# Gated Fourier and feed-forward mix: where the feed-forward share waits for the Fourier share, and when the first down step is loaded

## The chip, the cores and the metric

The kernel runs on one NeuronCore of one Trainium2 chip. The metric is the device time of one execution in microseconds (us), the median of several runs on the same chip. TensorE does the matrix products (PE in the profile; its weight loads are PEld), VectorE (DVE) and ScalarE (ACT) work on tiles in the on-chip memories, GpSimd (POOL) and SyncE (SP) here mostly issue transfers (DMAs) between these memories and the chip's main memory.

## The reference, cut to what matters

```python
def reference(A_x, A_dft_seq_re, A_dft_seq_im, A_dft_hid_re, A_dft_hid_im, B_x, B_w_gate, B_w_up, B_w_down, gate_w):
    def _A_ref(x, dft_seq_re, dft_seq_im, dft_hid_re, dft_hid_im):
        a = jnp.einsum("bsd,ed->bse", x, dft_hid_re)
        b = jnp.einsum("bsd,ed->bse", x, dft_hid_im)
        return jnp.einsum("ts,bse->bte", dft_seq_re, a) - jnp.einsum("ts,bse->bte", dft_seq_im, b)
    def _B_ref(x, w_gate, w_up, w_down):
        return (_gelu(x @ w_gate) * (x @ w_up)) @ w_down
    x = A_x
    g = _sigmoid((x * gate_w).sum(-1, keepdims=True))
    a = _A_ref(x, dft_seq_re, dft_seq_im, dft_hid_re, dft_hid_im)
    b = _B_ref(x, w_gate, w_up, w_down)
    return g * a + (1 - g) * b
```

x has 2048 tokens of 640 numbers, and the feed-forward part is 1728 wide. All is in 32-bit floats. The output is thus the sum of two shares: the Fourier share times g and the feed-forward share times 1 - g, with one g per token.

## The kernel before

**Tiles.** The 2048 tokens stand in four tiles of 512 (NT), worked in two pairs (tp = 0 and 1, t = 0 and 1 within a pair). The 640 columns are five blocks of 128 (the index e or d; ND = 5). The feed-forward width is 13 blocks of 128 and a rest of 64. A matrix product in 32-bit precision is done in three passes (`mm3`, L82): each operand is split into a high part, copied by ScalarE (`high`, L72), and a low part, which VectorE subtracts (`low`, L75); then TensorE does high by high (L84), high by low (L85) and low by high (L86). Many products are grouped into two-by-two schemes that save a product for some additions; their banks are called X, Z, V, L and Q, R, Y. TensorE's results land in eight banks of 128 x 512 in its accumulator memory (`bank`, L69). Operands take slots of 4 KB a partition out of 48 (`slot`, L63), small ones a tile out of 12 (`mtile`, L66).

**Stages.** First come the feed-forward blocks: a plain one and blocks f = 1 to 12, each for both pairs in seven steps (`gate_up`, L273). A step ends where the generator yields; in its steps VectorE adds or multiplies banks into the tiles s1, s2 and s5 (L298 after the third product bank V, L302 for X, L306 to L322 for the end), ScalarE applies the activation, and `keep` (L245) stores the hidden blocks and some differences of them to main memory, in hA and hT, from GpSimd's queue. At the end of block 11 the gates are worked out (`gate_rows`, L364), and the two tiles gm with 1 - g are loaded.

Then comes the down projection: 26 steps (`kseq`), for each pair seven with the products X, Z, V, L and seven with X, Q, R, Y; one in each second seven has nothing of its own to load. A step's weights (kw) and its two hidden halves (kr, 512 KB each, in two names that end in 0 and 1) are loaded by `load_k` (L450) from SyncE's queue; `split_k` (L478) makes their high parts kh and kb..h on ScalarE and their low parts kl and kb..l on VectorE; `step_k` (L535) does the products. Name 000 in kw000 or kb0000 is pair 0, first seven, step 0. When a bank set is complete, `put` (L541) multiplies a result by 1 - g and GpSimd stores it to accd, a scratch array in main memory for the feed-forward share.

Then follow the Fourier transform along the tokens (`cseq`; x parts xn loaded by `load_xn`, transform matrices by `load_c`, results u stored to uA and uT), and the one along the columns, with the output: 20 steps `useq`, five for each of pair 0 first half, pair 0 second half, pair 1 second half and, last, pair 1 first half. `fetch_mix` (L884) loads the tile gw with g and the pair's feed-forward share from accd into the tiles av; `mix` (L899) multiplies a result by g and adds it into av; `give` (L904) stores av to the output from GpSimd's queue. The last five steps are the part behind L987: `tail` (L991) runs the products of one bank over all five steps, so that the banks X, Z, V, L are ready one after the other, and each is multiplied, added into av and stored while the next one is worked out. The last bank is done in two halves, `yLast` being the second.

**What sets the order.** Each engine works through its instructions in program order. From `split_k(1)` on (L710), ScalarE and VectorE keep the order in which the code is written (`in_order`, L91). Ahead of it a scheduler orders each engine's instructions by what they wait for and by how early they are written. Work that is not urgent is put in a list `after` and written out at the next `late()`. SyncE's and GpSimd's transfers go out in their queues' order; a load into a slot waits until the slot's last reader is done.

**Where the first down step stands.** In block 12, `load_k(0)` to `load_k(2)` are written after steps 4 to 6 of the seven, `split_k(0)` after step 6; `split_k(1)` and `load_k(3)` follow when the block is written.

## Time and profile before

| | |
|---|---|
| runs | 1042.45, 1039.55, 1042.14 us; median 1042.14 us |
| profiled execution, first to last instruction | 1041.0 us |
| bytes read from and written to main memory | 173.93 MB, 63.98 MB |
| transfers of the hardware queue (issued by SyncE) | 174.22 MB |
| transfers of the software queue (issued by GpSimd) | 63.73 MB |

The profile is of one further execution. Its rows give, for a group of instructions of one line, engine and form, the busy time and mean duration; a row of a single instruction begins with its start in us from the span's start, then its duration, engine, line, operation and tiles (result <- operands). In brackets stands how long the engine stood idle just before it, and what it waited for. For a transfer there are three times in ns, for its issue, and then how long after issue it landed. "Granted clock" is the share of TensorE's full clock that it was given in the stretch.

### The profile page before, as it was taken

The page shows a single profiled execution, that of the slowest core. Times are in us where ns is not written, and L with a number is a line of the kernel's source. Part 1 is how long each engine was busy: PE and PEld are TensorE (multiplying, and loading weights), DVE is VectorE, ACT ScalarE, POOL GpSimd, SP SyncE. Part 2 cuts the span into 40 slices and gives each one's busy share as a digit, 9 for nine tenths or more (in the row PEclk, how much of TensorE's full clock was granted, in tenths as well). Part 3 has the DMA queues.
Part 4 walks back from the last instruction along what each step waited for, and adds up shares of the span by engine and source line. Part 5 has one row for each costly group of instructions (what it writes and reads, how often), then busy time and mean ns, then how long its engine had stood idle before and what let it go on. Part 6 is the DMA issues. An engine that isn't in the chain of part 4 may idle for free.

```text
span 1041.0 us, 12806 instructions
## 1 busy us (share of the span) xinstructions
PE 1026.8 (99%) x4523; PEld 848.6 (82%) x4523; DVE 785.4 (75%) x1051; ACT 448.8 (43%) x568; POOL 125.7 (12%) x237
## 2 busy tenths in 40 slices
PE   7999999999999899999999999999999999999997
PEld 5888888888888788888888888888888888888886
DVE  4898775767653966996798976696578769697888
ACT  5453333333532645655445443433344344354430
POOL 0012121212121200010010011001100200020011
PEclk9999999999999899999999999999999999999999
DMA  7146655647445977877866668467756777897762
GB/s 285 59 141 206 212 184 193 210 168 252 153 147 206 385 270 252 299 253 248 307 234 202 218 202 308 160 207 233 257 179 220 276 270 276 310 358 234 253 236 112
DMA packets 78753, 238.77 MB, mean 229 GB/s; under 512 B 10240, under 2 KB 18080, under 8 KB 78688
## 3 DMA queue, kind: packets, MB, share of 16 engines
q1 hardware_dynamic: 59408, 174.22, 49.4%
q0 software_dynamic: 19280, 63.73, 16.3%
q8 instruction: 35, 0.57, 0.2%
q14 instruction: 30, 0.25, 0.1%
HBM read 173.93 MB, written 63.98 MB: 229 GB/s over the span
## 4 chain that ended last, share of the span: by engine, by line
PE 65%; issue 21%; POOL 5%; DVE 5%; DMA 2%; ACT 1%; SPq 0%; POOLq 0%; ACTq 0%
PE pL L86 3%; PE pX L86 3%; PE pX L85 3%; PE pL L85 3%; PE pX L84 3%; PE pL L84 3%; POOL hA L246 2%; POOL hT L246 2%; PE pZ L86 1%; PE pV L86 1%; PE pY L86 1%; PE pY L85 1%; PE pR L86 1%; PE pR L85 1%; PE pQ L86 1%
## 5 line engine op out<-in xcount | busy, mean ns | idle before, releaser
L73 ACT ACTIVATE ch<-csa 128x1024 fp32r<-128x1024 f32 x32 | 34.0, 1062 | 88.8 <-DVE csa L431 53.7
L131 ACT ACTIVATE s<-pX 128x512 f32<-128x512 f32 x64 | 37.8, 596 | 73.2 <-PE pX L86 71.2
L73 ACT ACTIVATE ch<-cra 128x1024 fp32r<-128x1024 f32 x32 | 33.9, 1058 | 47.9 <-DVE cl L76 17.3
L76 DVE TENSOR_TENSOR cl<-cra,ch 128x1024 fp32r<-128x1024 f32 x32 | 39.1, 1222 | 17.6 <-ACT ch L73 16.8
L76 DVE TENSOR_TENSOR cl<-crb,ch 128x1024 fp32r<-128x1024 f32 x32 | 39.1, 1221 | 16.2 <-ACT ch L73 11.4
L85 PE MATMUL pL<-cl,xah 128*128 128x512 f32 x128 | 49.8, 389 | 0.0
L86 PE MATMUL pL<-ch,xal 128*128 128x512 f32 x128 | 49.8, 389 | 0.0
L298 DVE TENSOR_TENSOR s<-s,pV 128x512 f32<-128x512 f32 x24 | 16.3, 684 | 44.0 <-issue 24.4
L84 PE MATMUL pL<-ch,xah 128*128 128x512 f32 x128 | 49.3, 389 | 0.0
L246 POOL DMA_DIRECT2D hA<-s x48 | 26.0, 542 | 177.8 <-DVE s L308 171.4
L76 DVE TENSOR_TENSOR cl<-csb,ch 128x1024 fp32r<-128x1024 f32 x32 | 39.1, 1223 | 6.3 <-ACT ch L73 4.7
L73 ACT ACTIVATE ch<-crb 128x1024 fp32r<-128x1024 f32 x32 | 33.8, 1056 | 22.2 <-DVE cl L76 9.0
L76 DVE TENSOR_TENSOR cl<-csa,ch 128x1024 fp32r<-128x1024 f32 x32 | 39.1, 1222 | 4.0 <-ACT ch L73 3.3
L73 ACT ACTIVATE ch<-csb 128x1024 fp32r<-128x1024 f32 x32 | 33.9, 1059 | 11.9 <-PE pL L85 6.9
L76 DVE TENSOR_TENSOR kl<-kw,kh 128x1024 fp32r<-128x1024 f32 (+1 forms) x26 | 31.4, 1208 | 8.5 <-ACT kh L73 8.5
L307 ACT ACTIVATE s<-s 128x512 f32<-128x512 f32 x24 | 15.2, 634 | 39.1 <-DVE s L306 39.1
L73 ACT ACTIVATE kh<-kw 128x1024 fp32r<-128x1024 f32 (+1 forms) x26 | 27.3, 1048 | 7.8 <-DMA kw<-wsd 3.5
L299 ACT ACTIVATE s<-s 128x512 f32<-128x512 f32 x24 | 15.1, 630 | 31.7 <-DVE s L298 31.7
L85 PEld LDWEIGHTS pL<-cl,xah 128*128 128x128 f32 x128 | 24.0, 188 | 5.0
L84 PEld LDWEIGHTS pL<-ch,xah 128*128 128x128 f32 x128 | 24.0, 188 | 5.0
L86 PEld LDWEIGHTS pL<-ch,xal 128*128 128x128 f32 x128 | 24.0, 188 | 4.9
L771 POOL DMA_DIRECT2D uA<-s x16 | 8.6, 540 | 160.1 <-DVE s L817 153.3
(3564 smaller groups left out, 3356.8 us busy)
## 6 DMA issues: line engine op xcount, KB each, us to landing
cra<-in_ct SPq DMA_DIRECT2D x64, 512.0 KB, 4.1
crb<-in_ct SPq DMA_DIRECT2D x64, 512.0 KB, 4.7
hA<-s POOLq DMA_DIRECT2D x48, 256.0 KB, 4.4
hT<-s POOLq DMA_DIRECT2D x48, 256.0 KB, 5.4
kr<-hA SPq DMA_DIRECT2D x24, 512.0 KB, 7.8
kr<-hT SPq DMA_DIRECT2D x24, 512.0 KB, 6.5
ux<-uA SPq DMA_DIRECT2D x24, 512.0 KB, 5.2
ux<-uT SPq DMA_DIRECT2D x16, 512.0 KB, 5.6
```

What stands on the lines that cost most here:

```text
L73: nc.scalar.activation(hi, raw, AF.Copy)
L76: nc.vector.tensor_tensor(lo, raw, hi.bitcast(F32), op=ALU.subtract)
L84: nc.tensor.matmul(ps, lh, rh, start=first, stop=False, skip_group_check=True)
L85: nc.tensor.matmul(ps, lh, rl, start=False, stop=False, skip_group_check=True)
L86: nc.tensor.matmul(ps, ll, rh, start=False, stop=last, skip_group_check=True)
L131: nc.scalar.activation(m, src, AF.Copy)
L246: nc.gpsimd.dma_start(to[:, i], src)
L298: tt(s1, s1, V, op=ALU.add)
L299: nc.scalar.activation(s1, s1, AF.Gelu_apprx_tanh)
L307: nc.scalar.activation(s2, s2, AF.Gelu_apprx_tanh)
L771: nc.gpsimd.dma_start(to[:, i], src)
```

## The change

It does three things.

First, the feed-forward share is not kept in accd. `put` stores it directly into the output array, and accd goes.

Second, the Fourier share is put on by adding stores. `give` now multiplies a result by g, and GpSimd issues a store with `accum_op=ALU.add`, which adds the tile to what stands in the output. So the loads of av from accd and VectorE's additions into av go. Both tiles gw are loaded ahead of the output stage. In the last stage the results of bank X are added to the partial sums of pair 1 (ya, yc, ys), bank X itself is kept by a ScalarE copy (yx), Z and V are added to these, and each sum is multiplied by g and given by an adding store. Only the last column block (e = 4) of pair 1 is handled as before: its two tiles of feed-forward share are read back from the output into av (256 KB each), added on VectorE and stored plainly.

Third, `load_k(0)` is written at the end of block 11, right behind the loads of gm, `split_k(0)` after step 1 of block 12, and `load_k(1)` to `load_k(3)` after its steps 4 to 6.

```diff
--- before.py
+++ after.py
@@ -114,7 +114,6 @@
     uA, uT = ([[dram.tile([P, 4, T], F32, tag=f"u{n}{j}{p}", name=f"u{n}{j}{p}") for p in range(ND)] for j in range(2)] for n in "AT")
     grd, gmd = (dram.tile([1, S], F32, tag=n, name=n) for n in ("grd", "gmd"))
     wsd = [dram.tile([P, 8, P], F32, tag=f"wsd{k}", name=f"wsd{k}") for k in range(NK)]
-    accd = [dram.tile([P, ND, T], F32, tag=f"accd{t}", name=f"accd{t}") for t in range(NT)]
 
     def pair(dt, name):
         return slot(dt, [P, 2, T], name)
@@ -541,7 +540,7 @@
         def put(e, t, src):
             def do():
                 tt(src, src, gm[tp][:, t], op=ALU.mult)
-                nc.gpsimd.dma_start(accd[2 * tp + t][:, e], src)
+                nc.gpsimd.dma_start(out[2 * tp + t, e], src)
 
             after.append(do)
 
@@ -690,10 +689,11 @@
         for step in range(7):
             for w in work:
                 next(w)
-            if f == NF - 1 and step >= 4:
-                load_k(step - 4)
-                if step == 6:
+            if f == NF - 1:
+                if step == 1:
                     split_k(0)
+                if step >= 4:
+                    load_k(step - 3)
         if f % 2:
             sum_wd(f // 2)
         elif f <= 2 * ND:
@@ -701,6 +701,7 @@
         if f == NF - 2:
             gate_rows()
             gm = [gate_tile(gmd, tp, f"gm{tp}") for tp in range(2)]
+            load_k(0)
         for _ in range(2):
             if f > 1 and zq:
                 load_z(zq.pop(0))
@@ -709,7 +710,7 @@
     order.enter_context(in_order(ACT, DVE))
     split_k(1)
     for i in range(len(kseq)):
-        if i + 3 < len(kseq):
+        if 3 < i + 3 < len(kseq):
             load_k(i + 3)
         if i + 2 < len(kseq):
             split_k(i + 2)
@@ -881,34 +882,15 @@
 
     bk = {}
 
-    def fetch_mix(tp):
-
-        g = gate_tile(grd, tp, f"gw{tp}")
-        av = {}
-        for t in range(2):
-            for k in range(2):
-                a = pair(F32, f"av{tp}{t}{k}")
-                nc.sync.dma_start(a, accd[2 * tp + t][:, 2 * k : 2 * k + 2])
-                av[2 * k, t], av[2 * k + 1, t] = a[:, 0], a[:, 1]
-        a = pair(F32, f"av{tp}4")
-        for t in range(2):
-            nc.sync.dma_start(a[:, t], accd[2 * tp + t][:, 4])
-            av[4, t] = a[:, t]
-        return g, av
-
-    def mix(tp, e, t, v):
-        g, av = gav[tp]
-        tt(v, v, g[:, t], op=ALU.mult)
-        tt(av[e, t], av[e, t], v, op=ALU.add)
-
-    def give(tp, e, t):
-        nc.gpsimd.dma_start(out[2 * tp + t, e], gav[tp][1][e, t])
+    def give(tp, e, t, v):
+        tt(v, v, gw[tp][:, t], op=ALU.mult)
+        nc.gpsimd.dma_start(out[2 * tp + t, e], v, accum_op=ALU.add)
 
     def banks(names, n):
         for name in names:
             bk[name] = [bank(f"y{name}{n}{q}") for q in range(2)]
 
-    gav = {0: fetch_mix(0)}
+    gw = [gate_tile(grd, tp, f"gw{tp}") for tp in range(2)]
     for i, (tp, b, p) in enumerate(useq[: 3 * ND]):
         n = f"{tp}{b}"
         m = i - 2 * ND
@@ -944,11 +926,9 @@
 
             def mixed_y(tp=tp, cs=[sv["c11", q] for q in range(2)], ls=ls):
                 for q in range(2):
-                    mix(tp, 2 * q, 0, cs[q])
-                    give(tp, 2 * q, 0)
+                    give(tp, 2 * q, 0, cs[q])
                 for t in range(2):
-                    mix(tp, 4, t, ls[t])
-                    give(tp, 4, t)
+                    give(tp, 4, t, ls[t])
 
             after.append(mixed_y)
             continue
@@ -975,16 +955,15 @@
             for q in range(2):
                 s2, c21, c22 = es[q]
                 for e, t, v in ((2 * q, 1, s2), (2 * q + 1, 0, c21), (2 * q + 1, 1, c22)):
-                    mix(tp, e, t, v)
-                    if tp == 0:
-                        give(tp, e, t)
-
-        after.append(mixed_y)
-    last_mix = after.pop()
+                    give(tp, e, t, v)
+
+        if tp == 0:
+            after.append(mixed_y)
+    g = gw[1]
+    av = pair(F32, "av")
+    for t in range(2):
+        nc.sync.dma_start(av[:, t], out[2 + t, 4])
     late()
-    gav[1] = g, av = fetch_mix(1)
-    last_mix()
-    last = useq[3 * ND :]
     banks("XZVL", "last")
     Bs = [uks[3 * ND + p] for p in range(ND)]
 
@@ -996,19 +975,18 @@
     X, Z, V, L = (bk[name] for name in "XZVL")
     for q in range(2):
         tail(X[q], ("A11", q, True), 0)
-        x1, x2 = mtile(F32, f"yx1{q}"), mtile(F32, f"yx2{q}")
-        for t, v in ((0, x1), (1, x2)):
-            tt(v, X[q], g[:, t], op=ALU.mult)
-            tt(av[2 * q + 1, t], av[2 * q + 1, t], v, op=ALU.add)
-            give(1, 2 * q + 1, t)
-            tt(av[2 * q, t], av[2 * q, t], v, op=ALU.add)
+        s2, c21, c22 = es[q]
+        es[q] = copy(X[q], f"yx{q}"), s2
+        for t, v in enumerate((c21, c22)):
+            tt(v, v, X[q], op=ALU.add)
+            give(1, 2 * q + 1, t, v)
+        tt(s2, s2, X[q], op=ALU.add)
     for ps, w, b, t in ((Z, "S4", 3, 1), (V, "A12", 2, 0)):
         for q in range(2):
             tail(ps[q], (w, q, True), b)
-            v = mtile(F32, f"y{w}{q}")
-            tt(v, ps[q], g[:, t], op=ALU.mult)
-            tt(av[2 * q, t], av[2 * q, t], v, op=ALU.add)
-            give(1, 2 * q, t)
+            v = es[q][t]
+            tt(v, v, ps[q], op=ALU.add)
+            give(1, 2 * q, t, v)
     for t in range(2):
         parts = 2 if t else 1
         for c in range(parts):
@@ -1018,7 +996,7 @@
             tail(ps, ("e5", 1, False), 2 + t, cols)
             v = mtile(F32, f"yl{t}{c}")[:, : T // parts]
             tt(v, ps, g[:, t, cols], op=ALU.mult)
-            tt(v, v, av[4, t][:, cols], op=ALU.add)
+            tt(v, v, av[:, t, cols], op=ALU.add)
             (nc.sync if t else nc.gpsimd).dma_start(out[2 + t, 4, :, cols], v)
     order.close()
```

Behind line 117 the line numbers of the changed kernel are one lower, further back by 2 to 22.

VectorE at the end of block 12, before: s1, s2 and s5 are the block's tiles (the digits 12_0 and 12_1 are block and pair), pV, pX and pZ its banks, kl000 the low part of the first down step's weights and kb0000l that of its first hidden half.

```order
L298 TENSOR_TENSOR s112_0_2639<-s112_0_2639,pV12_0_2632 128x512
L298 TENSOR_TENSOR s112_1_2650<-s112_1_2650,pV12_1_2643 128x512
L302 TENSOR_TENSOR s512_2629<-s512_2629,pX12_0_2630 128x512
L302 TENSOR_TENSOR s512_2629<-s512_2629,pX12_1_2641 128x512
L306 TENSOR_TENSOR s212_0_2678<-s212_0_2678,pZ12_0_2631 128x512
L308 TENSOR_TENSOR s212_0_2678<-s212_0_2678,s512_2629 128x512
L306 TENSOR_TENSOR s212_1_2686<-s212_1_2686,pZ12_1_2642 128x512
L312 TENSOR_TENSOR s211_0_2509<-s212_0_2678,s211_0_2509 128x512
L314 TENSOR_TENSOR s511_2460<-s212_0_2678,s511_2460 128x512
L76 TENSOR_TENSOR kl000_2806<-kw000_2724,kh000_2805 128x1024
L308 TENSOR_TENSOR s212_1_2686<-s212_1_2686,s512_2629 128x512
L319 TENSOR_TENSOR s112_0_2639<-s112_0_2639,pX12_0_2630 128x512
```

The same place of the changed kernel:

```order
L297 TENSOR_TENSOR s112_0_2642<-s112_0_2642,pV12_0_2635 128x512
L76 TENSOR_TENSOR kl000_2676<-kw000_2625,kh000_2675 128x1024
L297 TENSOR_TENSOR s112_1_2653<-s112_1_2653,pV12_1_2646 128x512
L76 TENSOR_TENSOR kb0000l_2680<-kr0000_2628,kb0000h_2679 128x1024
L76 TENSOR_TENSOR kb0001l_2684<-kr0001_2630,kb0001h_2683 128x1024
L301 TENSOR_TENSOR s512_2632<-s512_2632,pX12_0_2633 128x512
L301 TENSOR_TENSOR s512_2632<-s512_2632,pX12_1_2644 128x512
L305 TENSOR_TENSOR s212_0_2693<-s212_0_2693,pZ12_0_2634 128x512
```

The low parts kl000, kb0000l and kb0001l stood behind the L308 and L322 operations of the block's end (kb0001l behind the rows shown); now all three stand ahead of the two additions of pX (L301).

ScalarE at the same place, before: copies of banks (L131, L291), the activations (L299, L307) and high parts (L73).

```order
L131 ACTIVATE s212_0_2678<-pX12_0_2630 128x512
L131 ACTIVATE s212_1_2686<-pX12_1_2641 128x512
L299 ACTIVATE s112_0_2639<-s112_0_2639 128x512
L299 ACTIVATE s112_1_2650<-s112_1_2650 128x512
L307 ACTIVATE s212_0_2678<-s212_0_2678 128x512
L73 ACTIVATE kh000_2805<-kw000_2724 128x1024
L307 ACTIVATE s212_1_2686<-s212_1_2686 128x512
L73 ACTIVATE kb0000h_2809<-kr0000_2727 128x1024
L73 ACTIVATE kb0001h_2813<-kr0001_2729 128x1024
```

ScalarE at that place now:

```order
L130 ACTIVATE s212_0_2693<-pX12_0_2633 128x512
L130 ACTIVATE s212_1_2701<-pX12_1_2644 128x512
L290 ACTIVATE s512_2632<-pZ12_0_2634 128x512
L290 ACTIVATE s512_2632<-pZ12_1_2645 128x512
L73 ACTIVATE kh000_2675<-kw000_2625 128x1024
L298 ACTIVATE s112_0_2642<-s112_0_2642 128x512
L73 ACTIVATE kb0000h_2679<-kr0000_2628 128x1024
L73 ACTIVATE kb0001h_2683<-kr0001_2630 128x1024
L298 ACTIVATE s112_1_2653<-s112_1_2653 128x512
```

The three high parts of the first down step, of which kh000 stood among the last activations and the others behind them, now stand around the activation of s1 (L298), ahead of both of s2 (L306).

VectorE in the last stage, at the first results of bank X, before: yx are products with g, av the feed-forward share that they are added into.

```order
L1001 TENSOR_TENSOR yx10_8203<-yXlast0_8180,gw1_8155 128x512
L1002 TENSOR_TENSOR av100_8157<-av100_8157,yx10_8203 128x512
L1004 TENSOR_TENSOR av100_8157<-av100_8157,yx10_8203 128x512
L1001 TENSOR_TENSOR yx20_8204<-yXlast0_8180,gw1_8155 128x512
L1002 TENSOR_TENSOR av110_8161<-av110_8161,yx20_8204 128x512
L1004 TENSOR_TENSOR av110_8161<-av110_8161,yx20_8204 128x512
L1001 TENSOR_TENSOR yx11_8228<-yXlast1_8181,gw1_8155 128x512
L1002 TENSOR_TENSOR av101_8159<-av101_8159,yx11_8228 128x512
L1004 TENSOR_TENSOR av101_8159<-av101_8159,yx11_8228 128x512
L1001 TENSOR_TENSOR yx21_8229<-yXlast1_8181,gw1_8155 128x512
L1002 TENSOR_TENSOR av111_8163<-av111_8163,yx21_8229 128x512
L1004 TENSOR_TENSOR av111_8163<-av111_8163,yx21_8229 128x512
```

The same place now:

```order
L981 TENSOR_TENSOR ya110_8098<-ya110_8098,yXlast0_8135 128x512
L886 TENSOR_TENSOR ya110_8098<-ya110_8098,gw1_7377 128x512
L981 TENSOR_TENSOR yc110_8113<-yc110_8113,yXlast0_8135 128x512
L886 TENSOR_TENSOR yc110_8113<-yc110_8113,gw1_7377 128x512
L983 TENSOR_TENSOR ys110_8096<-ys110_8096,yXlast0_8135 128x512
L981 TENSOR_TENSOR ya111_8101<-ya111_8101,yXlast1_8136 128x512
L886 TENSOR_TENSOR ya111_8101<-ya111_8101,gw1_7377 128x512
L981 TENSOR_TENSOR yc111_8116<-yc111_8116,yXlast1_8136 128x512
L886 TENSOR_TENSOR yc111_8116<-yc111_8116,gw1_7377 128x512
L983 TENSOR_TENSOR ys111_8099<-ys111_8099,yXlast1_8136 128x512
L988 TENSOR_TENSOR ys110_8096<-ys110_8096,yZlast0_8137 128x512
L886 TENSOR_TENSOR ys110_8096<-ys110_8096,gw1_7377 128x512
```

Each half of bank X had six operations, two products with g and four additions into av tiles; it now has five, two pairs of an addition and a product (each followed by an adding store) and a lone addition into ys, and the product for ys comes after Z is added (L988).

## The prediction

> **What bounds the kernel now.** I read the page's head first, then the busy time by stage, then the two stages that stand out.
>
> ```profile
> span 1041.0 us, 12806 instructions
> PE 1026.8 (99%) x4523; PEld 848.6 (82%) x4523; DVE 785.4 (75%) x1051; ACT 448.8 (43%) x568; POOL 125.7 (12%) x237
> PEclk9999999999999899999999999999999999999999
> ```
>
> TensorE is busy for 99% of the span, and its granted clock falls below the rest in one slice only, the fourteenth of 40 (338 to 364 us). So only time that TensorE loses can be won: where it is full, a shorter VectorE list or fewer loads are worth nothing. Two neighbouring stretches of 20 us, and 2 us pieces within the first (columns: stretch, then its length, then busy us and count for PE, PEld, DVE, ACT and POOL, then granted clock, DMA share, GB/s):
>
> ```profile
> 340.00:360.00 20.00, 16.90 (x63) 13.40 (x62) 19.30 (x24) 14.76 (x16) 5.43 (x10) 0.83 1.03 391
> 360.00:380.00 20.00, 20.00 (x90) 16.54 (x89) 18.71 (x22) 12.37 (x13) 0.00 (x0) 1.00 0.71 246
> 346.00:348.00 2.00, 0.20 (x1) 0.00 (x0) 2.00 (x4) 2.00 (x3) 1.69 (x4) 1.00 1.02 416
> 348.00:350.00 2.00, 0.70 (x2) 0.60 (x3) 2.00 (x4) 2.00 (x3) 0.86 (x2) 0.55 1.03 410
> 350.00:352.00 2.00, 2.00 (x6) 1.55 (x5) 2.00 (x2) 2.00 (x3) 0.66 (x2) 0.50 1.04 391
> 356.00:358.00 2.00, 2.00 (x11) 1.65 (x10) 2.00 (x3) 0.04 (x1) 0.00 (x0) 1.00 1.05 290
> ```
>
> A full stretch runs 90 matmuls; this one ran 63. 27 missing matmuls at 20/90 = 0.222 us are 6.0 us lost. The 2 us pieces show both parts: TensorE stands almost idle from 346 to 349, and then runs at half clock until about 355. What it waits for:
>
> ```profile
> 349.30 0.80 PE L85 MATMUL kX<-kb0000l,kh 128*128 128x512 f32 x1 [3.10 <-DVE kb0000l L76]
> 342.69 0.68 DVE L314 TENSOR_TENSOR s<-s,s 128x512 f32<-128x512 f32 x1
> 343.29 1.22 DVE L76 TENSOR_TENSOR kl<-kw,kh 128x1024 fp32r<-128x1024 f32 x1
> 347.44 0.68 DVE L319 TENSOR_TENSOR s<-s,pX 128x512 f32<-128x512 f32 x1
> 348.03 1.22 DVE L76 TENSOR_TENSOR kb0000l<-kr,kb0000h 128x1024 fp32r<-128x1024 f32 x1
> 349.77 1.22 DVE L76 TENSOR_TENSOR kb0001l<-kr,kb0001h 128x1024 fp32r<-128x1024 f32 x1
> 350.91 1.22 DVE L76 TENSOR_TENSOR kl<-kw,kh 128x1024 fp32r<-128x1024 f32 x1
> 340.76 1.04 ACT L73 ACTIVATE kh<-kw 128x1024 fp32r<-128x1024 f32 x1
> ```
>
> The first down step needs the low part of its hidden block, kb0000l, and VectorE gets to it only at 348.03, behind the element-wise end of the last feed-forward block (the L308 to L322 rows). It is queued late, not loaded late: the high part was free to start on ScalarE at 340.76. After 3.10 us of idling the half clock is a second cost of the same wait.
>
> The other place is the end:
>
> ```profile
> 1035.33 0.28 PE L86 MATMUL yLast<-ub191h,uw04l 128*128 128x256 f32 x1
> 1005.81 0.68 DVE L901 TENSOR_TENSOR ys<-ys,gw 128x512 f32<-128x512 f32 x1
> 1006.53 0.69 DVE L902 TENSOR_TENSOR av<-av,ys 128x512 f32<-128x512 f32 x1
> 1007.14 0.69 DVE L901 TENSOR_TENSOR ya<-ya,gw 128x512 f32<-128x512 f32 x1
> 1036.89 0.42 DVE L1020 TENSOR_TENSOR yl<-yLast,gw 128x256 f32<-128x256 f32 x1
> 1037.35 0.42 DVE L1021 TENSOR_TENSOR yl<-yl,av 128x256 f32<-128x256 f32 x1
> 1037.01 1.13 SPq L1022 DMA_DIRECT2D out<-yl  x2
> ```
>
> TensorE delivers its last result at 1035.33 + 0.28 = 1035.61, but VectorE has been behind since about 1006 and takes that result up at 1036.89 and ends at 1037.77. After that come one store and the end, 3.2 us that stay.
>
> **Part by part.**
>
> *First down step, one block earlier.* The new order on VectorE puts kl000, kb0000l and kb0001l between the two L298 additions and the two L302 additions of block 12, and ScalarE does kh000, kb0000h and kb0001h there too. When are their inputs there? SyncE issues its loads in the same order as now; only what they are counted under moves. The rows for the two hidden halves, and the first matmul that the moved work could delay:
>
> ```profile
> L475 SPq DMA_DIRECT2D kr<-hA x2: 382/524/665, 328.1 to 328.8; - x2
> DMA to landing us min/median/max: 7.3/7.6/7.8
> 337.47 0.69 DVE L302 TENSOR_TENSOR s<-s,pX 128x512 f32<-128x512 f32 x1 [0.67 <-PE pX L86]
> 341.28 0.39 PE L84 MATMUL pX<-xT04h,wa12h 128*128 128x512 f32 x1
> ```
>
> The halves were issued at 328.1 and 328.8 and landed 7.3 to 7.8 us later, the second at about 336.6. High part on ScalarE 1.04 us: 337.7. Low part on VectorE, 1.14 us from start to start (349.77 to 350.91): 337.8 to 338.9. Then the two L302 additions, 0.6 us apart: the first ends at about 339.6, the second at 340.2. The product that overwrites what the first one reads starts at 341.28, so 1.6 us are left; the second's comes nine matmuls (2.0 us) later. The feed-forward block is not delayed, and what stays of VectorE's list after it (the L314 operation at 342.69 and seven more, 0.6 us apart) ends near 347.5.
>
> The first down step then has all its operands by 339 and can follow at once on the last feed-forward matmul, 18 matmuls after 341.28, at 345.4. Its successor needs kl001 and two more low parts: 347.5 + 3 x 1.14 = 350.9, against a need at 345.4 + 30 x 0.227 = 352.2. So nothing of the gap reappears there. The gain is the whole 6.0 us: 3.1 us of standing, and the rest, 2.9 us, of half clock. [...]
>
> *Shares stored to the output.* Twenty stores change their target and nothing else; twelve loads of accd leave SyncE's queue, two loads of 256 KB come in, and the second gate tile is loaded right behind the first. In the output stage TensorE is full up to the end, so all of this hides behind it:
>
> ```profile
> av<-accd SPq DMA_DIRECT2D x8, 512.0 KB, 6.6
> av<-accd SPq DMA_DIRECT2D x4, 256.0 KB, 7.9
> ...
> 960.00:980.00 20.00, 20.00 (x90) 16.55 (x89) 17.19 (x21) 10.93 (x12) 0.00 (x0) 1.00 0.86 304
> ```
>
> The ten VectorE additions that go ahead of the last stage (0.69 us each) are worth nothing for the same reason, and a load that goes cannot cost. What could cost is the traffic that an adding store makes in its place; its bounds stand below.
>
> *Last stage by adding stores.* VectorE now does 38 operations after 1005.81; afterwards it does 24: ten for the X bank, eight for Z and V, six for L. The first ten, at 1.33 us for an addition and its product (1005.81 to 1007.14), end near 1012.4, where the Z bank is ready; from there each product waits for TensorE. So the last one starts when TensorE has delivered: 1035.61, 0.1 us to be noticed, 0.46 and 0.42 us for the two operations: 1036.6 instead of 1037.77, a gain of 1.2 us. ScalarE gets two copies of X, beside idle time. What is late next is TensorE itself.
>
> The trace has no adding store. Its bounds are the plain stores of the same size:
>
> ```profile
> L905 POOL DMA_DIRECT2D out<-av x18: 539/539/556, 952.5 to 1035.3; - x18
> DMA to landing us min/median/max: 1.9/2.3/5.4
> L544 POOL DMA_DIRECT2D accd<-ks x12: 539/539/548, 405.3 to 534.3; - x12
> DMA to landing us min/median/max: 3.6/7.1/9.7
> ```
>
> Its landing is bounded from below by 1.9 us (a gain is excluded, since nothing waits for such a store) and from above by 9.7 us, the slowest store beside full queues. I take 2.3 us, the nearest in place and size. GpSimd's own 0.54 us for the issue I keep. The last adding store follows the V bank:
>
> ```profile
> 1020.77 0.39 PE L84 MATMUL yVlast<-ub191h,uw04h 128*128 128x512 f32 x1
> ```
>
> That bank is done some 0.9 us later; with an addition and a product the store leaves at about 1023, less the 6.0 us won, 1017. Landing even 9.7 us later it is done at 1027, and the span ends near 1034. So either end costs nothing, as long as several can be under way together.
>
> **The sum.** 1041.0 - 6.0 - 1.2 = 1033.8 us of span. The runs of before lie at 1039.55 to 1042.45 with a median of 1042.14, which is 1.1 us above the profiled span. I take the difference off the median: 1042.14 - 7.2 = 1034.9 us.
>
> **Rivals.**
>
> *The moved operands hold up the block they were moved into.* For it speaks that only 1.6 us lie between the second half's landing, by way of four operations, and the product at 341.28, and that ScalarE and VectorE now stand in order behind those loads. Against it, the issue order and the traffic ahead of these loads are unchanged. If they land 2 to 4 us later, TensorE waits 0.4 to 2.4 us, and if that is enough for the half clock, up to 2.9 us more: 1035.3 to 1040.2. If the split ended so late that the gap stayed whole, 1040.9.
>
> *The lead is taken back later.* TensorE arrives 6 us earlier at every later step, and some step may be set by loads that do not come earlier. The tightest place:
>
> ```profile
> 478.55 0.85 ACT L73 ACTIVATE xah<-xn 128x768 fp32r<-128x768 f32 x1 [9.11 <-DMA xn<-in_xn]
> 483.79 0.39 PE L84 MATMUL kX<-kb1100h,kh 128*128 128x512 f32 x1
> 471.55 0.38 SPq L400 DMA_DIRECT2D xn<-in_xn  x1
> SPq L465 <- PE kL L86: 11.3, 1, 11.3
> ```
>
> ScalarE stands on the load of xn, and only then copies the X bank that TensorE needs at 483.79, with nothing to spare. But that load left SyncE just after an issue that had waited 11.3 us for TensorE, so it comes earlier with it. If it did not, up to the 6.0 us would go: 1034.9 to 1040.9.
>
> *The adding stores come one after the other and end the kernel late.* This is the one that ends slower. Eight of them leave in the last stage, the first near 1001 in the new time. If GpSimd's queue served one at a time, X us each, the last lands at 1001 + 8X. That passes the forecast's last store (1033) at X = 4, and is 0.3% slower than before from about X = 5.3; at X = 9.7 the span would be near 1080. Against it: plain stores of the size land in 2.3 us though one leaves for each L902 addition, every 1.33 us, so they overlap.
>
> That the change does not do what it says is no rival: the order of the rows shows the three splits ahead of the two additions, and TensorE's order otherwise as before.
>
> **Chances.** The forecast, 1033 to 1037: 0.72. Late operands: 0.12, half of it under 1039.0. Lead taken back: 0.08, half under 1039.0. Slow adding stores: 0.08, of which 0.05 over 1045.3 and 0.03 within. A measurement of this kernel can tell about 0.3%, 3.1 us, from no change. Faster by more: 0.72 + 0.06 + 0.04 = 0.82. Within: 0.06 + 0.04 + 0.03 = 0.13. Slower: 0.05. The range goes from 1032.0 (the lowest run of before lies 2.6 us under its median) to 1039.2, and leaves out the worst half of each rival.
>
> **What would show it.** Right: the stretch from 334 to 354 has 90 matmuls and a clock of 1.00, kb0000l ends before 341, and at the end the last L999 starts within 0.6 us of the last matmul's end. Wrong: a wait of PE pX for the L301 addition near 341; half clock anywhere after 15 us; PE waiting for ACT ks near 477; or the last adding store landing after the two stores of L1000. The prediction fails as a whole if TensorE's idle time only moves.

## The result and the profile after

| | before | changed |
|---|---|---|
| runs of the first comparison | 1042.45, 1039.55, 1042.14, 1040.30; median 1041.22 us | 1033.53, 1033.48, 1034.75, 1034.40; median 1033.97 us |
| ratio of the times | | 0.9938 (95% interval 0.9926 to 0.9950) |
| again, later | median 1040.76 us of 18 runs | median 1033.96 us of 6 runs; 0.9929 (0.9916 to 0.9943) |
| span of the profiled execution | 1041.0 us | 1031.8 us |

The change made the kernel 0.6 to 0.7% faster; the forecast was 1034.9 us in a range of 1032.0 to 1039.2. The profiled time stands 1.7 us over its span (1033.53 to 1031.8).

The page of the changed kernel, its head and clock:

```profile
span 1031.8 us, 12771 instructions
PE 1023.6 (99%) x4523; PEld 847.0 (82%) x4523; DVE 770.1 (75%) x1027; ACT 450.3 (44%) x570; POOL 131.9 (13%) x237
PEclk9999999999999999999999999999999999999999
```

The slice with the lowered clock is gone. Next, the busy time by stretch (columns as before), in the two places where the forecast looked:

```profile
334.00:354.00 20.00, 20.00 (x90) 16.59 (x89) 18.85 (x25) 13.44 (x15) 5.44 (x10) 1.00 1.03 407
346.00:348.00 2.00, 2.00 (x10) 1.68 (x9) 1.97 (x4) 2.00 (x3) 0.00 (x0) 1.00 1.04 413
348.00:350.00 2.00, 2.00 (x10) 1.65 (x10) 2.00 (x3) 2.00 (x3) 0.54 (x1) 1.00 1.03 380
1000.00:1020.00 20.00, 20.00 (x90) 16.59 (x89) 13.65 (x22) 1.20 (x2) 10.72 (x13) 1.00 1.01 147
```

From 334 to 354 TensorE runs its full 90 matmuls at full clock. The last line holds something new: the transfer engines are busy all the time (1.01) and yet move 147 GB/s, where in the first line they move 407. Single instructions of the same trace, in order of time:

```profile
335.04 1.23 DVE L76 TENSOR_TENSOR kb0000l<-kr,kb0000h 128x1024 fp32r<-128x1024 f32 x1 [0.29 <-ACT kb0000h L73]
337.53 1.28 DVE L301 TENSOR_TENSOR s<-s,pX 128x512 f32<-128x512 f32 x2
344.19 0.39 PE L85 MATMUL kX<-kb0000l,kh 128*128 128x512 f32 x1
1027.86 0.28 PE L86 MATMUL yLast<-ub191h,uw04l 128*128 128x256 f32 x1
1028.18 0.42 DVE L998 TENSOR_TENSOR yl<-yLast,gw 128x256 f32<-128x256 f32 x1 [2.71 <-PE yLast L86]
1028.64 0.43 DVE L999 TENSOR_TENSOR yl<-yl,av 128x256 f32<-128x256 f32 x1
1029.09 0.34 SPq L1000 DMA_DIRECT2D out<-yl  x1
```

The low part kb0000l is done at 336.3 and used at 344.19, 7.9 us later. At the end VectorE stands idle for 2.71 us and takes up the last bank as soon as TensorE delivers it. That TensorE is now the only limit also shows in the list of what it waits for, which has one line left, at the start of the kernel:

```profile
PE pm L84 <- ACT x011h L73: 4.6, 1, 4.6
```

The same wait was 5.8 us in the profiled execution of before (two waits). Where the 9.2 us between the two spans are: 1.4 us in that start (its first 20 us hold 44 matmuls before and 50 now, 6 more at 0.227 us), which differs from one execution to the next (the wait for the first pieces of x ended 6.5 to 8.2 us into the span in the profiles of this case); 6.1 us between 340 and 356 (the start of the last matmul moved by 7.47 us, from 1035.33 to 1027.86; less 1.4 us); and 1.7 us behind TensorE's last matmul, from 1041.0 - 1035.61 = 5.4 to 1031.8 - 1028.14 = 3.7 us.

### The profile page after: what moved, and what is told of

The parts are those of the page before. It is cut to its first block, busy times and chain, and to the rows that moved or that the text cites. A ratio compares the mean times of both kernels' runs of the same rounds, so it can differ in the third digit from the quotient of the medians.

```text
span 1031.8 us, 12771 instructions
## 1 busy us (share of the span) xinstructions
PE 1023.6 (99%) x4523; PEld 847.0 (82%) x4523; DVE 770.1 (75%) x1027; ACT 450.3 (44%) x570; POOL 131.9 (13%) x237
## 4 chain that ended last, share of the span: by engine, by line
PE 99%; DMA 0%; DVE 0%; ACT 0%; SPq 0%; issue 0%
PE pX L84 8%; PE pX L86 8%; PE pX L85 8%; PE pZ L86 5%; PE pZ L85 5%; PE pZ L84 5%; PE pV L86 3%; PE pV L85 3%; PE pV L84 3%; PE pL L86 3%; PE pL L84 3%; PE pL L85 3%; PE pY L86 1%; PE pQ L86 1%; PE pY L85 1%; PE pR L86 1%
## 5 line engine op out<-in xcount | busy, mean ns | idle before, releaser
L73 ACT ACTIVATE ch<-csa 128x1024 fp32r<-128x1024 f32 x32 | 34.0, 1063 | 89.3 <-DVE csa L430 54.3
L73 ACT ACTIVATE ch<-cra 128x1024 fp32r<-128x1024 f32 x32 | 33.9, 1058 | 46.9 <-PE pL L85 21.5
L73 ACT ACTIVATE ch<-crb 128x1024 fp32r<-128x1024 f32 x32 | 33.8, 1055 | 21.4 <-DVE cl L76 7.8
L73 ACT ACTIVATE ch<-csb 128x1024 fp32r<-128x1024 f32 x32 | 33.9, 1059 | 11.6 <-PE pL L85 6.6
L306 ACT ACTIVATE s<-s 128x512 f32<-128x512 f32 x24 | 15.2, 633 | 39.2 <-DVE s L305 39.2
L73 ACT ACTIVATE kh<-kw 128x1024 fp32r<-128x1024 f32 (+1 forms) x26 | 27.2, 1047 | 10.0 <-DMA kw<-wsd 5.7
L429 DVE TENSOR_TENSOR csa<-cra 128x512 f32<-128x512 f32 x32 | 22.0, 687 | 8.1 <-PE pL L85 6.5
```

Of the source, the lines that this page charges most:

```text
L73: nc.scalar.activation(hi, raw, AF.Copy)
L306: nc.scalar.activation(s2, s2, AF.Gelu_apprx_tanh)
L429: tt(s1[:, 0], r1[:, 1], r1[:, 0], op=ALU.subtract)
```

## The experiments

All times are medians of several runs, with those of the kernel before on the same chip beside them: 1040.46 us in the first group of four, 1039.89 in the second, 1040.76 in the third. The changed kernel itself ran again in the third group only (1033.96 us); a kernel of the first two is compared with its first comparison (1033.97 us), so tenths of such a difference mean little.

### One part of the change at a time

The kernel before with nothing but the early load and split of the first down step:

```diff
-            if f == NF - 1 and step >= 4:
-                load_k(step - 4)
-                if step == 6:
-                    split_k(0)
+            if f == NF - 1:
+                if step == 1:
+                    split_k(0)
+                if step >= 4:
+                    load_k(step - 3)
...
+            load_k(0)
...
-        if i + 3 < len(kseq):
+        if 3 < i + 3 < len(kseq):
```

> Theory A (the first down step's low parts stood too late on VectorE, and the half clock came of that wait): all of the wait and of the half clock goes, 6.2 us, so about 1035.0 us against 1041.2 before; VectorE's backlog at the end stays, its last addition 2.2 us behind TensorE's last matmul. Rival B (the gain comes from the 5 MB of loads that go with accd, and from VectorE's additions): within 1 us of before.

Measured: 1036.23 us, ratio 0.9957 (0.9945 to 0.9970), 4.2 us faster. What TensorE waits for in its trace is this alone:

```profile
PE pm L84 <- ACT x011h L73: 5.8, 2, 4.6
```

and its end, in order of time:

```profile
1030.26 0.42 DVE L1022 TENSOR_TENSOR yl<-yLast,gw 128x256 f32<-128x256 f32 x1
1030.37 1.13 SPq L1024 DMA_DIRECT2D out<-yl  x2
1030.71 0.42 DVE L1023 TENSOR_TENSOR yl<-yl,av 128x256 f32<-128x256 f32 x1
```

The wait is gone and VectorE's backlog stays: its last operation ends at 1031.13, 2.2 us behind the end of TensorE at 1028.95. So this part alone carries most of the gain, but the time gained 4.2 us, not the 6.2 that were expected.

The other half: the changed kernel with the load and split where they were.

```diff
-            if f == NF - 1:
-                if step == 1:
-                    split_k(0)
-                if step >= 4:
-                    load_k(step - 3)
+            if f == NF - 1 and step >= 4:
+                load_k(step - 4)
+                if step == 6:
+                    split_k(0)
...
-            load_k(0)
...
-        if 3 < i + 3 < len(kseq):
+        if i + 3 < len(kseq):
```

> Theory A: the wait of 3.1 us and the half clock near 350 stay, the end gains 1.2 to 1.7 us, so 1039.5 to 1040.0 us. Rival B: 1034 to 1036 us, with a shorter wait near 350.

Measured: 1038.77 us, 0.9981 (0.9972 to 0.9991), 1.7 us faster. With the 4.2 us of the other half that makes 5.9 us. Rival B is out: without accd's loads and VectorE's additions nothing changes at the wait. TensorE's wait there:

```profile
PE kX L85 <- DVE kb0000l L76: 3.1, 1, 3.1
```

and the stretches around it:

```profile
340.00:360.00 20.00, 16.89 (x75) 13.66 (x74) 19.55 (x23) 15.44 (x17) 5.44 (x10) 1.00 1.04 393
348.00:350.00 2.00, 1.12 (x5) 0.95 (x6) 2.00 (x3) 2.00 (x4) 1.08 (x2) 1.00 1.02 401
350.00:352.00 2.00, 2.00 (x11) 1.62 (x10) 2.00 (x3) 2.00 (x3) 0.54 (x1) 1.00 1.04 393
```

This is the surprise of the study. The wait is the same, 3.1 us, but the granted clock stays at 1.00: 75 matmuls in the 20 us, where the profile of before had 63. The half clock does not have to follow this wait.

### The load or the split

The changed kernel, loading early as it does, but splitting late.

```diff
-                if step == 1:
+                if step == 6:
                     split_k(0)
```

> The changed kernel with the first down step loaded early as it is, but its split written after step 6 of the last block, as before. Theory A (place of the split decides): the wait of 3.1 us and the half clock are back, 6 us slower than the changed kernel, about 1040 us. Rival C (the early load decides): stays at 1034 us.

Measured: 1038.31 us, 0.9978 (0.9968 to 0.9987), 4.3 us over the changed kernel. The wait is back at its full 3.1 us (and again without half clock in the profiled execution), so the early load alone is worth nothing that can be told (the kernel with neither took 1038.77 us) and the place of the split everything; rival C is out. The size was again less than expected. A second wait appears in this profile, 130 us later:

```profile
PE kX L85 <- DVE kb0000l L76: 3.1, 1, 3.1
PE kX L84 <- ACT ks L130: 0.5, 1, 0.5
```

It is the tight place near 477 of the forecast, where ScalarE stands on a load of x parts and copies bank X late. It costs 0.2 to 0.8 us in six of the 14 profiles of this case, all of kernels with the changed stores, and under 0.1 us in the others, that of before among them.

### How long a wait costs the clock

If the half clock does not belong to the wait as such, its length should matter. A longer wait, by writing the first split behind the second:

```diff
-                if step == 1:
-                    split_k(0)
...
     split_k(1)
+    split_k(0)
```

> The changed kernel with the first down step's split written behind that of the second, so three more low parts stand ahead of it. Wait of TensorE about 6.8 us. Theory D (the clock falls by chance after 3.1 us of idling, and always after a clearly longer one): half clock in every run, some 2.9 us more, so 1034 + 6.8 + 2.9 = 1043.5 us with a narrow spread. If the fall has nothing to do with the length: 1041 us in most runs and 1043.5 in a quarter.

Measured: 1043.63 us (1043.03 to 1044.74, 10 runs), 9.7 us over the changed kernel on the same chip. The mean granted clock was 0.995 or 0.997 in all ten. TensorE's waits near 350:

```profile
PE kX L85 <- DVE kb0000l L76: 4.4, 1, 4.4
PE kX L84 <- ACT kb0000h L73: 2.1, 1, 2.1
PE kZ L84 <- ACT kb0001h L73: 0.2, 1, 0.2
```

They are 6.7 us, so 3.0 us are left. The half clock of this profile (6.8 us, below) explains about 2.0 of them: TensorE stood for 2.8 us of it anyway, and 4.0 us at half speed lose 2.0. The rest is not traced further; in the kernel with the stores alone a wait without half clock also cost a little more than its length, 15 matmuls or 3.3 us for 3.1.

A shorter wait, by splitting the weights early and the two hidden halves late:

```diff
+            if i == 0:
+                h, l = first_w
...
                 if step == 1:
-                    split_k(0)
+                    first_w = slot(F32R, [P, 8, P], "kh000"), slot(F32R, [P, 8, P], "kl000")
+                    split(*first_w, kraw[0][0])
+                if step == 6:
+                    split_k(0)
```

> The changed kernel with the weights of the first down step split early, its two hidden halves after step 6: wait of TensorE about 2 us. Theory D: never half clock, so 1034 + 2 = 1036 us without an upper cluster. If the fall has nothing to do with the length: a quarter of the runs near 1039.

Measured: 1036.43 us (1035.23 to 1039.14, 7 runs). Six runs had a mean clock of 1.000, and one, the slowest by 1.7 us, 0.998: "never" was wrong, "seldom" fits. The waits of its profile:

```profile
PE kX L85 <- DVE kb0000l L76: 2.0, 1, 2.0
PE kX L84 <- ACT ks L130: 0.4, 1, 0.4
```

The kernel before lies between the two. Of its 49 runs beside these experiments, 15 had a mean clock of 0.997 or less (1039.99 to 1043.23 us), the other 34 had 0.998 or more (1038.46 to 1041.19 us). In the 18 of the third group the two kinds stand apart: 1041.85 to 1043.23 us and 1038.46 to 1041.19 us.

The mean clock has to be read with care, since it also counts what comes after the last matmul. In the profile of before the clock falls a second time there, to 0.51 on average from 1037.6 to 1041.0, which is worth up to 0.0016 in the mean. So 0.997 or less in a run of before says that the clock fell at the wait, and 0.998 (21 of the 34) does not say either way. The kernels with the changed end, 3.6 us instead of 5.4 behind the last matmul, tell more. Without the wait, none of 21 runs had less than 0.999 (the changed kernel, the one with plain stores and the last one below). With the wait of 3.1 us (stores alone, split late), 10 of 23 runs had 1.000, 10 had 0.998 and three 0.996 or 0.997. So there is a level between: 0.998 of some 1037 us is, by an estimate from these means, about 4 us of half clock (0.002 x 1037 / 0.5), shorter than the 6.8 us in the profile of before.

Where the clock falls and rises can be read from short stretches of before:

```profile
347.00:348.00 1.00, 0.00 (x0) 0.00 (x0) 1.00 (x2) 1.00 (x2) 0.84 (x2) 1.00 1.04 423
348.00:348.50 0.50, 0.00 (x0) 0.00 (x0) 0.50 (x2) 0.50 (x2) 0.00 (x0) 0.68 1.00 406
354.00:355.00 1.00, 1.00 (x3) 0.73 (x3) 1.00 (x2) 0.91 (x1) 0.00 (x0) 0.50 1.08 426
355.00:356.00 1.00, 1.00 (x6) 0.81 (x5) 1.00 (x2) 0.15 (x1) 0.00 (x0) 1.00 0.99 385
```

and of the kernel with the long wait:

```profile
349.00:350.00 1.00, 0.00 (x0) 0.00 (x0) 1.00 (x2) 1.00 (x2) 0.11 (x1) 0.80 1.03 375
350.00:351.00 1.00, 0.00 (x0) 0.00 (x0) 1.00 (x2) 1.00 (x2) 0.34 (x1) 0.50 1.03 395
355.00:356.00 1.00, 1.00 (x4) 0.71 (x4) 1.00 (x2) 0.00 (x0) 0.00 (x0) 0.50 1.14 276
356.00:357.00 1.00, 1.00 (x5) 0.81 (x4) 1.00 (x2) 0.00 (x0) 0.00 (x0) 0.79 1.00 269
```

A mean of 0.68 over half a microsecond, between 1 and 0.5, puts the fall at 348.2; the rise is at 355.0. In the second kernel the fall is at 349.6 and the rise at 356.4. Both lie 6.8 us apart, though TensorE came back 1.1 us after the fall in the one and 2.8 us after it in the other. So in these two the half clock lasted equally long, and a later return spent more of it idle.

Why the same 3.1 us of waiting cost the clock in some executions and not in others was not shown, but the traces give a lead. Each records when the granted clock changed. In that of before it is 1.00 from 13.68 us on, 0.50 from 348.18 to 355.01, 1.00 again up to 1037.67 and 0.50 behind that: stretches of 334.51, 6.827 and 682.67 us, which are 49, 1 and 100 times 6.827 us. In that of the changed kernel it is 1.00 from 11.67 to 1032.26, just behind the end of the span, which is 1020.59 us or 149.5 times 6.827. So in these two traces the changes lie whole multiples of 3.413 us apart, half of 6.827. TensorE's idle time in stretches of this length, counted back from a fall:

| kernel | stretch, us | idle in it, us | clock behind it |
|---|---|---|---|
| before | 344.77 to 348.18 | 1.98 | falls |
| before | 1034.26 to 1037.67 | 2.07 | falls |
| long wait | 342.77 to 346.19 | 1.70 | stays |
| long wait | 346.19 to 349.60 | 2.18 | falls |
| changed | 1025.43 to 1028.85 | 0.71 | stays |

Laid on to the whole trace, the other stretches of before have at most 1.12 us of idling from 13.68 us on. So in these profiles the clock fell behind the stretches with 1.98, 2.07 and 2.18 us of idling, and behind none with 1.70 us or less. That it is not the length of a wait that counts but how much of it lies in one such stretch is the author's reading of these few falls; no run here moved a stretch on purpose. By it, as an estimate, 3.1 us cut in two can leave as little as 1.55 us on each side, under the 1.70 that cost no clock, and a wait of 2.0 us (one run in seven) would have to lie nearly whole in one stretch.

### What an adding store costs

The changed kernel with plain stores in the place of the 18 adding ones.

```diff
-        nc.gpsimd.dma_start(out[2 * tp + t, e], v, accum_op=ALU.add)
+        nc.gpsimd.dma_start(out[2 * tp + t, e], v)
```

> Leaves out the addition in the 18 stores of the Fourier share (they overwrite). If adding stores cost nothing on the path that sets the end: within 0.5 us of the changed kernel, about 1034 us, though the last of these stores lands some 2.3 us after its issue instead of 4.9, and ScalarE's copies of bank X no longer wait. If they hold up the end: 1 to 3 us faster than the changed kernel.

Measured: 1034.29 us, 0.9940 (0.9926 to 0.9953), as the changed kernel (span 1031.8 in both). So the adding stores cost no time here. But they are not as cheap as plain ones. The changed kernel's stores from 999 on, with their issue times on GpSimd and the idle time before them:

```profile
999.44 0.85 POOL L887 DMA_DIRECT2D out<-ys  x1 [45.69 <-DVE ys L886]
1000.04 1.15 POOL L887 DMA_DIRECT2D out<-ya  x1
1000.64 1.44 POOL L887 DMA_DIRECT2D out<-yc  x1
1003.64 0.86 POOL L887 DMA_DIRECT2D out<-ys  x1 [1.56 <-issue]
1006.12 0.86 POOL L887 DMA_DIRECT2D out<-ya  x1 [1.62 <-DVE yc L981]
1007.41 0.87 POOL L887 DMA_DIRECT2D out<-yc  x1 [0.43 <-DVE ys L983]
```

For all fourteen, from issue to landing (in us):

```profile
DMA to landing us min/median/max: 3.9/4.8/6.5
```

The same six with plain stores:

```profile
999.47 0.54 POOL L887 DMA_DIRECT2D out<-ys  x1 [52.70 <-DVE ys L886]
1000.09 0.54 POOL L887 DMA_DIRECT2D out<-ya  x1
...
1002.56 0.54 POOL L887 DMA_DIRECT2D out<-yc  x1
```

their landing, and the stretch from 1000 to 1020:

```profile
DMA to landing us min/median/max: 2.3/2.6/3.2
```

```profile
1000.00:1020.00 20.00, 20.00 (x90) 16.57 (x89) 13.77 (x22) 1.20 (x2) 7.04 (x14) 1.00 0.50 185
```

All six results are ready by 1002.0 (VectorE's products, 0.6 us apart). The plain stores go out as fast as GpSimd issues them. The adding ones come to a stop after three: the first three land at 1003.3, 1005.8 and 1007.1, and the fourth, fifth and sixth start at 1003.64, 1006.12 and 1007.41, each 0.3 us after one of these landings. (For two of them the profile names VectorE, L981 and L983, as what ended the wait, but their own results were ready long before.) From there to the fourteenth, which lands at 1025.9, one lands each 1.74 us ((1025.9 - 1003.3) / 13). The transfer engines are busy twice as long in this stretch (1.01 against 0.50), though fewer bytes pass in it (147 GB/s against 185), and GpSimd takes 0.86 us instead of 0.54 to issue one. What hides it: the last product of a result for these stores ends at 1016.0, and the last plain store lands at 1030.8, 4.9 us behind the last adding one. One more effect is hidden too. ScalarE's copies of bank X (yx) take tiles that the first adding stores still read:

```profile
1003.44 0.60 ACT L130 ACTIVATE yx<-yXlast 128x512 f32<-128x512 f32 x1 [11.23 <-DMA out<-ys]
```

The bank was complete at 997.2. VectorE, behind it, still ends its work on X, Z and V at 1016.0, 5 us before bank L is there at 1021.0.

To see the price, the eight results of pair 1 are given twice,

```diff
-        nc.gpsimd.dma_start(out[2 * tp + t, e], v, accum_op=ALU.add)
+        for _ in range(1 + tp):
+            nc.gpsimd.dma_start(out[2 * tp + t, e], v, accum_op=ALU.add)
```

> Adds each of pair 1's eight results to the output twice (16 stores instead of 8, so its Fourier share counts double there). Theory A (adding stores pass one after the other, one each 1.7 us): 22 of them from 999 on end near 1040, the span near 1041 to 1043 against 1031.8. If they overlap as the plain ones do: span unchanged within 1 us.

or in two halves by columns (each row of 2 KB in two pieces of 1 KB),

```diff
-        nc.gpsimd.dma_start(out[2 * tp + t, e], v, accum_op=ALU.add)
+        for h in range(1 + tp):
+            c = slice(h * T // 2, (h + 1) * T // 2 if tp else T)
+            nc.gpsimd.dma_start(out[2 * tp + t, e][:, c], v[:, c], accum_op=ALU.add)
```

> Each of pair 1's eight adding stores cut in two by columns (twice the stores and twice the pieces of a row, same bytes). If the price goes by bytes: landings end near 1026 as in the changed kernel, the span stays at 1032. If by store or by piece: as with the stores given twice, span 1041 to 1043.

or in two halves by partitions (64 whole rows each).

```diff
-        nc.gpsimd.dma_start(out[2 * tp + t, e], v, accum_op=ALU.add)
+        for h in range(1 + tp):
+            r = slice(h * P // 2, (h + 1) * P // 2 if tp else P)
+            nc.gpsimd.dma_start(out[2 * tp + t, e][r], v[r], accum_op=ALU.add)
```

> Each of pair 1's eight adding stores cut in two by partitions (twice the stores, same pieces of a row, same bytes). If the price goes by store: span 1041 to 1043. If by piece or by byte: landings end near 1026, span 1032.

One profiled execution of each:

| kernel | span, us | last adding store lands | from TensorE's end to the span's end | us per result of 256 KB |
|---|---|---|---|---|
| changed | 1031.8 | 1025.9 | 3.7 | 1.74 |
| given twice | 1045.2 | 1043.1 | 16.8 | 1.88 a store |
| halves by columns | 1036.3 | 1034.2 | 6.5 | 2.51 |
| halves by partitions | 1032.6 | 1027.3 | 3.6 | 1.65 |

The last column is the distance of the landings (of pair 1's in the last two rows). In the second row four stores also waited for an earlier store to the same place, 5.3 us in all, so 1.88 us is rather too high; in the last row the 0.8 us more of span are a wait near 477, and its end is that of the changed kernel. Given twice, the stores end the kernel, 13 us late: the rival of the forecast that ends slower, with 8 more stores instead of a price of 4 us and more each. Twice as many stores with the same rows cost nothing (1.65 us against 1.74), and twice as many pieces cost nearly half as much again (2.51). So between these kernels the price did not go by the number of stores. Why cut rows cost more, and why the fourth store waited for the first to land, was not shown.

Last, the place where such a store would not be hidden: the last column block given by adding stores as well, which saves its load and a VectorE operation for each piece.

```diff
-    av = pair(F32, "av")
-    for t in range(2):
-        nc.sync.dma_start(av[:, t], out[2 + t, 4])
...
-            tt(v, v, av[:, t, cols], op=ALU.add)
-            (nc.sync if t else nc.gpsimd).dma_start(out[2 + t, 4, :, cols], v)
+            nc.gpsimd.dma_start(out[2 + t, 4, :, cols], v, accum_op=ALU.add)
```

> The changed kernel, with the last column block of pair 1 given by adding stores from GpSimd too (no av, one VectorE operation less for each of the three pieces). Theory A (an adding store takes about 2 us longer from issue to landing than a plain one, which counts only behind the last matmul): 0.4 us less on VectorE, some 2 us more for the last landing, so 1.5 to 2.5 us slower than the changed kernel, 1035.5 to 1036.5 us. If adding stores are as quick as plain ones: about 0.4 us faster, 1033.6 us.

Measured: 1036.21 us (1035.00 to 1037.45), 0.9960 (0.9946 to 0.9974), 2.2 us over the changed kernel. Its end, the span being 1035.7:

```profile
1030.43 0.42 DVE L995 TENSOR_TENSOR yl<-yLast,gw 128x256 f32<-128x256 f32 x1 [3.17 <-PE yLast L86]
1031.26 0.87 POOL L996 DMA_DIRECT2D out<-yl  x1 [2.40 <-DVE yl L995]
```

This store lands at 1034.6, 3.3 us after its issue, against 1.7 us for the plain one from SyncE; from TensorE's end to the span's end it is 5.3 us instead of 3.7. Not all of this is the addition's, since the store also moved from SyncE's queue to GpSimd's: there it starts 0.4 us after VectorE's result, and a plain store of the larger size took 2.3 us from GpSimd (the kernel with plain stores). So by an estimate from these rows 1.0 us of the longer landing is the addition's (3.3 against 2.3) and 0.6 the queue's (2.3 against 1.7). Either way the change is right to read this block back.

### The changed kernel again, and one step further

> The changed kernel once more, on the chip of the three below. About 1034 us; no run over 1036, since without the wait near 345 no run can lose the half clock (before: clusters near 1040.3 and 1042.5 us).

Measured: 1033.29 to 1034.09 us in six runs, all with a mean clock of 1.000; the kernel before spread over 4.8 us on the same chip.

```diff
-XN_AT = [5, 10, 15, 20]
+XN_AT = [5, 10, 15, 19]
```

> The changed kernel with the fourth load of x parts written one down step earlier (XN_AT 19 instead of 20), ahead of four loads of 1.5 MB. If the waits of 0.1 to 0.8 us at the bank X of step 21, seen in most profiles, come from that load: they go, 0.2 to 0.5 us faster than the changed kernel, too little to be told from it by the time alone. Otherwise unchanged, or slower where the four loads passed are now late.

Measured: 1033.55 us (1033.37 to 1034.24), 0.9928 (0.9914 to 0.9943). In its trace ScalarE copies bank X at 469.9 and TensorE needs it at 476.2, so the wait that this load caused is gone, and no other has come. The 0.4 us against the changed kernel cannot be told from no change by these times.

## Why the prediction was right, point by point

**First down step.** Right in mechanism and place. The three splits stood where the order showed them, the two L301 additions ended at 338.2 and 338.8, before TensorE needed their banks at 339.9 and 341.9 (1.7 us, forecast 1.6, and 3.1), and the gap did not come back with the next step. In the profiled executions the gain was 6.1 us, against 6.0 forecast.

**The size for the measured time.** Here one term was wrong: "The gain is the whole 6.0 us: 3.1 us of standing, and the rest, 2.9 us, of half clock." The part alone was worth 4.2 us in the median. The 3.1 us of standing are in every profile of a kernel with the late split, so at most 1.1 us are left for the clock, not 2.9. The half clock is not in every run. Of the 49 runs of before, 15 show it for certain (0.997 or less), 13 show none (0.999 or 1.000), and the profiled execution happened to be one of the dearest, with 0.995. From a single profile the two costs cannot be told apart; three runs that lay at 1039.55, 1042.14 and 1042.45 could have warned that something came and went. Two readings of the clock were off as well. The fall came 2.0 us into the wait (348.2, after TensorE stopped at 346.2), so it did not take 3.1 us of idling. And the half clock did not run from 349 to about 355 but lasted 6.8 us, from 348.2 to 355.0; TensorE worked in 5.7 of these, and half of that is the 2.9 us.

**The base.** The forecast took its gain off a median of 1042.14 us, and two of those three runs were above 1041.9, where only 12 of the 49 later ones lay. So the base was some 1.5 us too high, and the gain of 7.2 us was 0.4 to 1.0 us too large for the medians measured later (1040.76 to 1033.96 is 6.8 us, and 1040.46 to the 1034.29 of the kernel with plain stores 6.2). The first comparison itself gives 7.2 us. The two errors go opposite ways, so that the time came within 1 us is luck in part.

**The end.** Forecast 1.2 us, measured 1.7 us, in the profiles and in the kernel that has only the stores. 1.23 us are VectorE's backlog, as forecast, though from too short a list of operations (next point) (its last operation ends 0.93 us behind TensorE instead of 2.16; it takes up the last bank 0.04 us after TensorE's end, 1028.14 to 1028.18, where the forecast put 0.1). The other half microsecond lies behind VectorE: 3.23 us to the end of the span before, 2.73 now. 0.14 of it is the last landing (1.85 and 1.71 us after its issue), the rest, 0.35 us, lies behind the last landing; what it is stays open.

**Adding stores.** Right that they cost nothing, but for a narrower reason than given. "2.3 us, the nearest in place and size" was half of what such a store takes, 4.8 us; "as long as several can be under way together" held for three of them; and the argument against the slow rival, that plain stores overlap, did not carry over. And two counts were short, because the six results of pair 0 that are also written out there were left out. From 1005.81 on VectorE has 50 operations before, not 38, and 30 in the changed kernel from the same place on, not 24; and not eight adding stores leave from 1001 on but fourteen from 999.4. So such stores, one after the other, pass the forecast's last store, 1033, from 2.4 us each ((1033 - 999.4) / 14), not from 4. They took 1.74 us, and the conclusion held with much less room than the forecast saw. Their slack at the end is 4.9 us, less than three stores.

**The rivals.** Late operands: not seen. The lead taken back: not in the changed kernel's profile, though waits of up to 0.8 us stand at that place in others. That a rival was in sight there was right; the forecast's reason against it (the load leaves SyncE behind TensorE and comes earlier with it) holds only when the transfer does not get longer, from 6.4 us in the changed kernel to 7.3 us in the one with the stores alone.

## What to carry to other kernels

A wait of TensorE can be priced twice, by its length and by the clock. Here the second price differed from run to run (the clock fell in one of seven runs with a wait of 2.0 us, in ten of ten with 6.7 us): take it from several runs with their mean clocks, not from one profile. Compare mean clocks only between kernels with the same end, since the stretch behind the last matmul counts too (the kernel that gives the stores twice has 0.994 without any such wait). To move an operand's preparation, look for the place where its engine waits for its own inputs anyway; here the order on VectorE was worth all, and the earlier load alone nothing that could be told. An adding store spares an engine's addition and a load, but count its time: here, at 256 KB a store and three under way, one landed each 1.74 us, so it belongs where work of that length still follows, and not behind the last result.

## What the runs showed of the hardware that was not expected

- After a wait of 3.1 us TensorE's clock fell in some executions and not in others; after 6.7 us of waits it fell in ten of ten runs, after 2.0 us in one of seven. In the profiles of before and of the changed kernel its changes lie whole multiples of 3.413 us apart (2, 98, 200 and 299). The two falls that were profiled in the middle of a kernel lasted 6.8 us.
- The stores that add into main memory kept the transfer engines twice as busy as plain ones (1.01 against 0.50 of the same stretch, at 147 GB/s against 185), landed in 4.8 us instead of 2.6, took GpSimd 0.86 us to issue instead of 0.54, and with 128 rows of 2 KB only three were under way at a time.
- Cutting rows of 2 KB in two made an adding store half as dear again (2.5 us against 1.7 per 256 KB); cutting the same store into two sets of whole rows did not (1.65 us).
